# A down-projection by seven products instead of eight

## The chip, the core and the metric

The kernel runs on one core of a Trainium2 chip. The engines are TensorE (PE in the profile), which multiplies matrices, VectorE (DVE) and ScalarE (ACT), which work on elements and read PE's results, GpSimd (POOL), which works on SBUF alone and issues the DMAs that convert types, and SyncE (SP), which issues the others. PE writes into PSUM, eight banks of 512 f32 in each of 128 partitions. The metric is the device time of one execution in microseconds (us); less is better.

## The reference

```
state = gamma * state + k_t v_t^T;  y_t = scale * q_t state        # for each batch (4) and head (8), 768 steps
x  = y as 3072 tokens x 512
xn = x / sqrt(mean(x*x) + 1e-6) * rms_g
out = (silu(xn @ w_gate) * (xn @ w_val)) @ w_out                   # 512 -> 1536 -> 512
```

Inputs and output are f32. A retention layer is followed by a gated feed-forward layer.

## The kernel before

The 768 steps are cut into six chunks `c` of 128 steps; with the four batches `b` a chunk has 512 tokens. Inside a chunk the recurrence becomes a masked product of q and k (operations `A` for the scores, `M0` and `M1` for the mask on DVE, `Y` for the product with v and with the state of the chunks before), and the state is carried from chunk to chunk (`K` the new part on PE, `U` the sum on DVE, `B` a bf16 copy on POOL). `S` and `R` give the norm of each token, `N` scales the rows, and `X` with `XE` or a transposing DMA (`XE` on SP) turns them into `xnT[c]`, with the model dimension on the partitions.

The feed-forward layer then works on 12 blocks `n` of 128 hidden units: `g` and `v` are the gate and value products, four matmuls of 512 tokens for a block (`L549`); `s` is silu on ACT (`L559`); `h` multiplies both on DVE into `hT[c]` (`L567`), 12 blocks x 512 tokens in bf16, of which there are two buffers. The down-projection `d` takes `hT[c]` of one batch (128 tokens) as the stationary operand and a row block of `wo_b` (512 columns) as the moving one, 12 matmuls into one bank (`L574`). `o` copies the bank into SBUF, on DVE or ACT, and `st` stores it (`L587`). For the last batch of the last chunk `e` does the same in three column pieces (`L596`). So the down-projection has 6 x 4 x 12 matmuls of 512 columns, the last 12 of them cut in three.

`H` and `hot` are matmuls of ones, which compute nothing (`L240`, `L234`). `Lq`, `Lk`, `Lv`, `wg`, `wv` and `wo` are loads; `Cq` and `Ck` turn loaded q and k into bf16, `V` does so for v, `D` scales k, `Tq`/`Tk` with `Eq`/`Ek` or `tq`/`tk` transpose.

The order of all this is one string, `ORDER`, written out ahead of the kernel. A word is an operation, its indices, behind `@` its engine (D, A, P, S), and behind `/` its banks: `h.5.0.1.0.4` is chunk 5, block 0 to 1, batches 0 to 4. Each engine takes its instructions in the order of the string, and waits for those of other engines by semaphores, so the string settles what stands behind what in each queue. A bank or a buffer is used again as soon as its last reader is done.

Of the kernel before, what the change touches and what calls it, by code (L numbers as in the profile page):

```python
# [22 lines left out]
N.0.0 M0.0.3 Y.0.1/1 H.1/2 X.0.0/4 J.0.3/7 wv.2.4 S.0.1 XE.0.0@D U.0.0@A R.0.2 R.0.1 Ck.1.1@A N.0.2 B.0.0 H.2/2
Y.0.3/0 g.0.0.2.0.1/2 K.0.2/6 S.0.3 s.0.0.2.0.1 N.0.1 U.0.2@A wg.4.6 X.0.2/4 R.0.3 XE.0.2@D D.0.1@D
v.0.0.2.0.1/3 X.0.1/2 wv.4.6 causal XE.0.1@A Lk.1.2@P v.0.0.2.2.3/4 wg.6.9 Lq.1.2@P wv.6.9 h.0.0.2.0.1
g.0.0.2.2.3/6 D.0.3@D Lq.1.0@P g.0.0.2.1.2/5 g.0.2.3.0.3/3 s.0.0.2.2.3 h.0.0.2.2.3 s.0.0.2.1.2 g.0.3.4.0.3/6
N.0.3 v.0.0.2.1.2/4 D.1.1@D Tq.1.1/5 Lk.1.0@P Tk.1.1/0 X.0.3/7 Eq.1.1@D K.0.1/2 wg.9.12 v.0.3.4.0.3/1 Lv.1.1@P
# [607 lines left out]
```

## Time and profile before

| | |
|---|---|
| three timed runs | 233.72, 233.92, 234.96 us; median 233.92 |
| the profiled execution, first to last instruction (its span) | 233.6 us |
| mean granted PE clock | 0.993 |
| instructions that count as work | PE 1771, DVE 241, ACT 231, POOL 163 |

The profile is one execution; for it there is no time but its span. The busy table gives for each engine the time with an instruction at work, and the slices the same in 40 equal pieces (9 is 90% or more). The chain is followed back from the last instruction, at each step to what released it. In rows of groups, the numbers behind the first bar are the busy time in us and the mean duration in ns, and behind the second the idle time before the group and who ended it. In rows of the timeline and of the chain, the first number is the start and the second the length, in us. A matmul's row in the timeline lasts longer than its share of the stream, since neighbours overlap; the chain counts from end to end.

### The profile page before, as it was taken

To read this page: it belongs to the slowest core of one execution; us is meant where nothing else is said; L and a number is where in the kernel's file an instruction comes from. 1 tells how busy PE (TensorE), PEld (TensorE's weight loads), DVE (VectorE), ACT (ScalarE), POOL (GpSimd) and SP (SyncE) were. 2 spreads that over 40 slices of the span, in tenths; PEclk is the share of its full clock that TensorE was granted. 3 is DMA by queue.
4 is the path that set the end of the run, shared out by engine and by line. 5 is a ranking of instruction groups with operands and counts; after the bars stand their busy time and mean duration, and the time that the engine had idled before them with its cause. 6 is when DMAs were issued, how large, how long until landed. Compare 5 with 4: busy or idle time off the path is not lost.

```text
span 233.6 us, 4637 instructions
## 1 busy us (share of the span) xinstructions
PE 227.6 (97%) x1771; PEld 120.8 (52%) x1771; DVE 130.4 (56%) x241; ACT 96.1 (41%) x231; POOL 89.7 (38%) x163
## 2 busy tenths in 40 slices
PE   8799999999999999999999999999999999999994
PEld 2458855645545655445554444554455444444444
DVE  6479639753662965628975239866367532323320
ACT  7658433514337231464731346553265332232202
POOL 8958998550544555030273741247003100000000
PEclk9979999999999999999999999999999999999999
DMA  7999999999798888999988899968511400020222
GB/s 126 147 180 123 127 179 184 205 145 215 133 206 214 171 194 140 262 218 221 235 173 146 179 221 206 198 149 142 148 61 27 112 0 0 3 90 9 83 89 93
DMA packets 105353, 33.61 MB, mean 144 GB/s; under 512 B 94449, under 2 KB 102385, under 8 KB 105330
## 3 DMA queue, kind: packets, MB, share of 16 engines
q1 hardware_dynamic: 81858, 25.70, 50.2%
q0 software_dynamic: 23472, 7.60, 30.1%
q8 instruction: 14, 0.23, 0.4%
q14 instruction: 9, 0.07, 0.1%
HBM read 28.31 MB, written 6.29 MB: 148 GB/s over the span
## 4 chain that ended last, share of the span: by engine, by line
PE 89%; DMA 4%; POOL 2%; ACT 2%; DVE 1%; issue 0%; SPq 0%; POOLq 0%; DVEq 0%; ACTq 0%
PE v_ps L549 27%; PE g_ps L549 27%; PE o_ps L574 21%; PE a_ps L403 3%; DMA kb<-in_k_dram 3%; PE y_ps L441 2%; PE kv_ps L526 2%; PE y_ps L445 2%; DMA out_dram<-o_sb 1%; PE o_ps L596 1%; PE hot_ps L240 1%; PE t_ps L366 1%; PE t_ps L371 1%; PE xt_ps L495 1%; ACT xsq L455 1%; ACT xsq L458 1%
## 5 line engine op out<-in xcount | busy, mean ns | idle before, releaser
L567 DVE TENSOR_TENSOR hT<-sg,v_ps 128x512 bf16<-128x512 bf16 (+2 forms) x76 | 48.7, 656 | 47.8 <-PE v_ps L549 34.8
L549 PE MATMUL v_ps<-xnT,wv_b 128*128 128x512 bf16 (+2 forms) x344 | 71.2, 345 | 0.1
L559 ACT ACTIVATE sg<-g_ps 128x512 bf16<-128x512 f32 (+2 forms) x76 | 42.1, 575 | 70.6 <-PE g_ps L549 68.1
L549 PE MATMUL g_ps<-xnT,wg_b 128*128 128x512 bf16 (+2 forms) x344 | 70.0, 344 | 0.0
L574 PE MATMUL o_ps<-wo_b,hT 128*128 128x512 bf16 x276 | 63.5, 379 | 0.0
L549 PEld LDWEIGHTS <-wg_b 128*128 128x128 bf16 x344 | 30.4, 98 | 29.3
L549 PEld LDWEIGHTS <-wv_b 128*128 128x128 bf16 x344 | 30.2, 98 | 28.9 <-DVE am L426 0.6
L574 PEld LDWEIGHTS <-hT 128*128 128x128 bf16 x276 | 26.3, 98 | 29.1
L468 POOL TENSOR_SCALAR ms<-ssq 128x1 f32<-128x1 f32 x24 | 4.6, 190 | 59.1 <-ACT xsq L458 58.4
L426 DVE TENSOR_TENSOR am<-a_ps,causal 128x512 bf16<-128x512 f32 x32 | 20.6, 685 | 7.8 <-PE a_ps L403 7.5
L339 POOL TENSOR_TENSOR qb<-qf,ydec 128x512 bf16<-128x512 f32 x13 | 14.0, 1074 | 25.2 <-DMA qf<-in_q_dram 24.9
L146 ACT COPY o_sb<-o_ps 128x512 f32<-128x512 f32 (+1 forms) x16 | 8.8, 552 | 29.7 <-PE o_ps L574 23.1
L458 ACT ACTIVATE xsq<-y_ps 128x512 f32<-128x512 f32 x22 | 13.2, 599 | 18.9 <-PE y_ps L445 13.7
L482 DVE SCALAR_TENSOR_TENSOR xn<-y_ps,rstd,g_bc 128x512 bf16<-128x512 f32 x22 | 16.3, 748 | 4.3 <-POOL rstd L470 3.0
L146 DVE COPY o_sb<-o_ps 128x512 f32<-128x512 f32 (+1 forms) x10 | 6.4, 648 | 18.1 <-PE o_ps L574 12.2
L541 POOL CAST st_b<-st_f 64x256 bf16<-64x256 f32 x40 | 15.9, 398 | 1.3
L470 POOL TENSOR_TENSOR rstd<-ms,mhalf 128x1 f32<-128x1 f32 x24 | 13.3, 552 | 2.0
L534 DVE TENSOR_TENSOR st_f<-st_f,kv_ps 128x512 f32<-128x512 f32 x16 | 10.8, 684 | 5.2 <-PE kv_ps L526 4.6
L356 ACT ACTIVATE vp<-vf,vdec 128x64 bf16<-128x64 f32 x48 | 12.2, 343 | 0.0
L426 DVE TENSOR_TENSOR am<-a_ps,mask 128x512 bf16<-128x512 f32 x16 | 10.4, 686 | 2.5 <-PE a_ps L403 2.3
L240 PE MATMUL hot_ps<-one 128*128 128x512 bf16 x20 | 8.5, 547 | 1.1 <-DVE one L153 1.1
L441 PEld LDWEIGHTS <-am 128*128 128x128 bf16 x176 | 7.8, 99 | 3.1 <-issue 0.3
(99 smaller groups left out, 174.8 us busy)
## 6 DMA issues: line engine op xcount, KB each, us to landing
out_dram<-o_sb SPq DMA_DIRECT2D x23, 256.0 KB, 2.4
kf<-in_k_dram SPq DMA_DIRECT2D x18, 256.0 KB, 3.8
qf<-in_q_dram SPq DMA_DIRECT2D x16, 256.0 KB, 3.9
vf<-in_v_dram SPq DMA_DIRECT2D x16, 256.0 KB, 3.9
wo_b<-in_moe_w_out_dram POOLq DMA_DIRECT2D x3, 512.0 KB, 12.2
qb<-in_q_dram POOLq DMA_DIRECT2D x8, 128.0 KB, 6.6
vp<-in_v_dram POOLq DMA_DIRECT2D x8, 128.0 KB, 6.5
kb<-in_k_dram POOLq DMA_DIRECT2D x6, 128.0 KB, 5.9
```

What stands on the lines that cost most here:

```text
L146: (e.copy if e is ACT else e.tensor_copy)(out, in_)
L339: e.tensor_tensor(out=u["qb"], in0=u["qf"], in1=ydec[:, c, :, None].to_broadcast([128, H, D]), op=ALU.mult)
L426: DVE.tensor_tensor(out=u["am"][:, i], in0=u["a"][i], in1=m, op=ALU.mult)
L441: nc.tensor.matmul(y[:, h, :], u["am"][:, h % 2, h // 2, :], u["vp"][:, h, :], start=h == 0, stop=c == 0 and h == H - 1, skip_group_check= ...
L458: ACT.activation(xsq, flat(u["y"]), AF.Square, accum_out=u["ssq"])
L470: POOL.tensor_tensor(out=u["rstd"], in0=ms, in1=mhalf, op=ALU.pow)
L482: DVE.scalar_tensor_tensor(out=u["xn"], in0=flat(u["y"]), scalar=u["rstd"], in1=g_bc, op0=ALU.mult, op1=ALU.mult)
L541: POOL.tensor_copy(st_b[b][r, :, i * 64:i * 64 + 64], st_f[b][r, :, i * 64:i * 64 + 64])
L549: nc.tensor.matmul(p[:, (n - n0) * m:(n - n0 + 1) * m], W[w][0][:, s, n * 128:(n + 1) * 128], xnT[c][:, s, b0 * C:b1 * C], start=s == 0, s ...
L559: ACT.activation(sg[:, :cols], done["wg", c, n0, b0][:, :cols], AF.Silu)
L567: DVE.tensor_tensor(out=hT[c][:, n0:n1, b0 * C:b1 * C], in0=sg, in1=p, op=ALU.mult)
L574: nc.tensor.matmul(o_ps[c, b], hT[c][:, n, b * C:(b + 1) * C], wo_b[:, n, :], start=n == 0, stop=n == NFF - 1)
```

## The change

For chunks 1 to 5 the down-projection is done by one level of Strassen's method. The left operand, a chunk's 512 tokens x 1536 hidden units, is split in two halves of tokens (batches 0 and 1, `LO`; 2 and 3, `HI`) and two halves of hidden units, and `w_out` in two halves of hidden units and two of columns. The halves of hidden units are interleaved: of each four blocks the first two (`J0`) and the last two (`J1`). Instead of eight products of quarters there are seven; each, for a group of 128 tokens `p` (0 or 1), has six matmuls of 256 columns. They go two to a bank (`ma`, `mb`, `md`) or alone (`m1`; `m6` and `m7` for the very last).

Their left operands are sums of quarters, made for each third `r` of the hidden units: `z1` and `z2` into buffers of their own, `z3` and `z4` in place in `hT`. The right operands `w1`, `w6`, `w7` are made once in buffers, `w3` and `w4` in place in `wo_b`, behind the plain down-projection of chunk 0. The products are put together by `cb` and `c1` (copies out of PSUM), `p1` and `pu` (sum and difference of `ma` with `cb`), `pv` (adds `c1`) and `p2` (adds `md`), and `s1` and `s2` store two halves of 256 columns at a time.

For the room in SBUF, `hT` becomes five buffers of a third of a chunk each; the `w` sums take turns with the masks of chunks 0 and 1 in three buffers (`wide`); `z2` takes turns with `qdec` and `g_row` in four (`mid`), `z1` with `kd`, and the outputs `o1` and `o2` with `o_sb` in five; the squares `xsq` become bf16 with one buffer. The identity is made apart from `pick`. The string `ORDER` is new from end to end: also the loads, the head and the fillers stand in another order. The diff, with the parts of the string that are spoken of below:

```diff
--- before
+++ after
...
-d.5.2.0.12/3 e.5.3.1/0 o.5.1@D st.4.2@S st.5.0@S st.5.1@S e.5.3.2/7 o.5.2@A st.5.2@S o.5.3.2@D st.5.3.2@S
...
+Lk.0.2@S rms.1@S Lq.0.0@P Lq.0.2@P Lq.0.1@P Lk.0.0@P iota Lk.0.1@P ident H.8/0 Ck.0.2@D pick mk1 Lq.0.3@P mk0 vd
+D.0.2@D Tq.0.0/1 Lv.0.2@P Lk.0.3@P G/2 GE@A Lk.1.3@P Tk.0.2/3 Tq.0.2/4 Ek.0.2@D Tk.0.0/5 Lv.0.1@P Tq.0.1/6 Lv.0.3@P
...
+Cq.2.0@P o.0.2@A w7@P w1@P U.1.0@D B.1.0 d.0.1.0.4/7 s.1.10.11.0.4 h.1.8.9.0.4 h.1.1.2.0.3 d.0.0.0.4/3 s.1.2.3.0.3
+A.2.2/1264 M1.2.3 d.0.0.4.8 d.0.1.4.8 tq.2.0 g.1.6.7.0.4/5 M1.2.2 s.1.6.7.0.4 M0.2.3 M0.2.2 d.0.1.8.12 V.2.0@D
+d.0.0.8.12 B.1.1 tk.2.1 Lv.2.1@S A.2.0/4261 o.0.1@D V.2.2@A v.1.2.3.0.3/5 M0.2.1 M1.2.1 B.1.2 M1.2.0 V.2.1@P Lv.2.3@S
+h.1.2.3.0.3 M0.2.0 Y.2.2/7 S.2.2 g.1.3.4.0.3/6 V.2.3@P Y.2.1/1 v.1.6.7.0.4/2 S.2.1 Lk.3.3@S R.2.2 Ck.3.3@P s.1.5.6.0.4
...
+v.1.3.4.0.3/2 h.1.3.4.0.3 z2.1.0@D s.1.9.10.0.4 XE.2.1@S XE.2.3@S Cq.3.3@P Cq.3.2@P v.1.9.10.0.4/6 K.2.3/4 XE.2.0@S
+Lq.4.1@S z1.1.0@D g.1.4.5.0.4/5 K.2.0/2 h.1.9.10.0.4 Lk.3.0@S g.1.7.8.0.4/7 V.3.3@P U.2.3@D Lq.3.1@S v.1.7.8.0.4/6
...
+s.2.9.10.0.4 Lq.4.3@S Lq.4.0@S Cq.4.3@P U.2.0@D v.2.9.10.0.4/7 U.2.2@D z4.1.1@D h.2.9.10.0.4 h.2.7.8.0.4 g.2.6.7.0.4/2
+s.2.6.7.0.4 v.2.5.6.0.4/6 h.2.5.6.0.4 tk.3.3 mb.1.0/3 tq.3.3 Lv.3.1@S mb.1.1/0 tk.3.1 tk.3.0 A.3.2/7426 w3@D cb.1.0@D
+h.2.6.7.0.4 Cq.4.1@D V.3.1@A z4.1.2@D M0.3.3 Lk.4.2@S Lv.3.0@S M1.3.3 B.2.3 Cq.3.1@P B.2.1 B.2.2 g.2.0.1.0.4/3
+g.2.10.11.0.4/5 M0.3.2 M1.3.2 cb.1.1@A s.2.10.11.0.4 g.2.11.12.0.4/0 tq.3.0 v.2.10.11.0.4/2 U.3.3@D g.2.8.9.0.4/6
+tq.3.1 h.2.10.11.0.4 Lq.5.2@S Lk.4.1@S z3.1.1@D z2.2.1@D A.3.0/7541 M1.3.1 B.2.0 s.2.0.1.0.4 V.3.2@A z3.1.0@P
+s.2.8.9.0.4 v.2.8.9.0.4/3 Y.3.2/2 K.3.1/6 Y.3.3/1 M0.3.0 Lq.5.3@S S.3.2 w4@P g.2.2.3.0.4/7 s.2.2.3.0.4 S.3.3 M1.3.0
+M0.3.1 st.0.2@S Ck.4.1@A h.2.8.9.0.4 V.3.0@P Y.3.0/5 Cq.5.2@D K.3.0/4 Ck.5.1@A z1.1.2@D ma.1.0/3 s.2.11.12.0.4 tk.4.0
+Lv.4.3@S tq.4.1 U.3.1@D Y.3.1/7 R.3.2 N.3.2 g.2.1.2.0.4/6 R.3.3 p1.1.0 st.0.1@S pu.1.0 z3.1.2@D ma.1.1/2 v.2.0.1.0.4/0
+S.3.1 Lk.4.3@S st.0.3@S st.0.0@S N.3.3 S.3.0 R.3.0 Ck.4.2@D U.3.0@D v.2.11.12.0.4/3 md.1.0/1 Cq.4.0@D R.3.1 N.3.1
+h.2.11.12.0.4 XE.3.2@S XE.3.3@S N.3.0 pu.1.1 XE.3.1@S md.1.1/4 v.2.3.4.0.4/7 Ck.4.3@P z1.1.1@P m1.1.1/3 p1.1.1
+z3.2.1@P h.2.0.1.0.4 B.3.3 V.4.3@A K.4.3/5 U.4.3@D Lv.4.1@S V.4.1@P XE.3.0@S Lq.4.2@S s.2.1.2.0.4 K.3.2/6
+v.2.2.3.0.4/2 g.2.3.4.0.4/0 s.2.3.4.0.4 h.2.2.3.0.4 U.3.2@D h.2.3.4.0.4 Lv.5.2@S Lv.4.2@S Lk.5.2@S Lq.5.0@S m1.1.0/5
+c1.1.1@D pv.1.1@D Cq.4.2@D c1.1.0@A v.2.1.2.0.4/2 h.2.1.2.0.4 g.3.8.9.0.4/6 s.3.8.9.0.4 p2.1.1 V.4.2@P B.3.1 z4.2.1@D
+g.3.2.3.0.4/0 s1.1.0@S v.3.0.1.0.4/7 Cq.5.3@D v.3.1.2.0.4/3 z2.2.2@D pv.1.0@P z4.2.2@D g.3.1.2.0.4/5 s.3.1.2.0.4
+h.3.1.2.0.4 v.3.8.9.0.4/6 h.3.8.9.0.4 Lv.5.1@S p2.1.0 g.3.0.1.0.4/2 g.3.11.12.0.4/4 K.4.2/5 tk.4.3 s.3.11.12.0.4
...
+h.5.7.8.0.4 z1.5.2@D g.5.4.5.0.4/5 v.5.6.7.0.4/0 z1.4.1@D s.5.6.7.0.4 h.5.6.7.0.4 g.5.5.6.0.4/1 v.5.5.6.0.4/4
+s.5.4.5.0.4 s.5.5.6.0.4 h.5.5.6.0.4 v.5.4.5.0.4/6 h.5.4.5.0.4 z2.5.1@D z3.5.0@D m1.4.1/7 z2.5.2@P z3.5.2@P c1.4.1@A
+z3.5.1@D z4.5.2@D pv.4.1@D p2.4.1 m1.4.0/5 z4.5.1@D c1.4.0@A ma.5.0/0 pv.4.0@D s2.4.1@S s1.4.0@S mb.5.0/1 cb.5.0@A
+p2.4.0 p1.5.0 s1.5.0@S pu.5.0 mb.5.1/4 cb.5.1@A ma.5.1/6 p1.5.1 z1.5.0@P z1.5.1@P m1.5.0/7 s2.4.0@S s1.5.1@S c1.5.0@A
+pu.5.1 pv.5.0@P md.5.0/5 m1.5.1/2 c1.5.1@A p2.5.0 hot.2/1 m6.5.1/3 m7.5.1/4 s2.5.0@S pv.5.1@D p2.5.1.1 s2.5.1.1@S
+p2.5.1.0 H.3/0 hot.3/7 s2.5.1.0@S H.3/6 H.1/1
 """
...
+    def wide(name):
+        return sb.tile([128, 1024], F32, name=name, tag="wide", bufs=3)
+
+    def mid(shape, dtype, name):
+        return sb.tile(shape, dtype, name=name, tag="mid", bufs=MID)
...
-    mask0 = const.tile([128, 2, NHP, C], F32, name="mask0")
-    mask1 = const.tile([128, 2, NHP, C], F32, name="mask1")
-    qdec = const.tile([128, NHP, C], F32, name="qdec")
+    mask0 = wide("mask0").rearrange("p (i hp j) -> p i hp j", i=2, hp=NHP)
+    mask1 = wide("mask1").rearrange("p (i hp j) -> p i hp j", i=2, hp=NHP)
+    qdec = mid([128, NHP, C], F32, "qdec")
...
-    g_row = const.tile([1, DM], F32, name="g_row")
+    g_row = mid([128, DM], F32, "g_row")[0:1]
...
-        xsq = ring([128, DM], F32, "xsq", 2)
+        xsq = ring([128, DM], BF16, "xsq", 1)
...
+    def h_of(c, r):
+        if (c, r) not in hT:
+            hT[c, r] = ring([128, 4, GT], BF16, "hT", HB)
+        return hT[c, r]
...
-    def o(e, bk, c, b, i=None):
-        p = o_ps[(c, b) if i is None else (c, b, i)]
-        if ("o", c, b) not in done:
-            done["o", c, b] = ring([128, DM], F32, "o_sb", 4)
-        copy(e, done["o", c, b] if i is None else done["o", c, b][:, CUT[i]:CUT[i + 1]], p)
-
-    @op
-    def st(e, bk, c, b, i=None):
-        m = slice(0, DM) if i is None else slice(CUT[i], CUT[i + 1])
-        e.dma_start(out=out_v[c, b][:, m], in_=done["o", c, b][:, m])
-
-
-    CUT = (0, 192, 384, 512)
-
-    @op
-    def e(e, bk, c, b, i):
-        p = o_ps[c, b, i] = bank(bk[0], [128, CUT[i + 1] - CUT[i]], F32, "o_ps")
-        for n in range(NFF):
-            nc.tensor.matmul(p, hT[c][:, n, b * C:(b + 1) * C], wo_b[:, n, CUT[i]:CUT[i + 1]],
-                             start=n == 0, stop=n == NFF - 1)
+    def o(e, bk, c, b):
+        done["o", c, b] = ring([128, DM], F32, "o_sb", OB)
+        copy(e, done["o", c, b], o_ps[c, b])
+    @op
+    def st(e, bk, c, b):
+        e.dma_start(out=out_v[c, b], in_=done["o", c, b])
+    wo_q = wo_b.rearrange("p (r j i) m -> p r j i m", j=2, i=2)
+    HM = DM // 2
+    def block(j, m):
+        return wo_q[:, :, j, :, m * HM:(m + 1) * HM]
+    def wsum(i, e, j0, m0, j1, m1, how):
+        if i in (3, 4):
+            x = block(j0, m0)
+        else:
+            x = wide("w%d" % i)[:, :NFF * HM // 4].bitcast(BF16).rearrange("p (r i m) -> p r i m", i=2, m=HM)
+        e.tensor_tensor(out=x, in0=block(j0, m0), in1=block(j1, m1), op=how)
+        done["w", i] = x
+    F["w1"] = lambda e, bk: wsum(1, e, 0, 0, 1, 1, ALU.add)
+    F["w3"] = lambda e, bk: wsum(3, e, 0, 1, 1, 1, ALU.subtract)
+    F["w4"] = lambda e, bk: wsum(4, e, 1, 0, 0, 0, ALU.subtract)
+    F["w6"] = lambda e, bk: wsum(6, e, 0, 0, 0, 1, ALU.add)
+    F["w7"] = lambda e, bk: wsum(7, e, 1, 0, 1, 1, ALU.add)
+    LO, HI = slice(0, GT // 2), slice(GT // 2, GT)
+    J0, J1 = slice(0, 2), slice(2, 4)
+    @op
+    def z1(e, bk, c, r):
+        h = hT[c, r]
+        done["z1", c, r] = sb.tile([128, 2, GT // 2], BF16, name="sA", tag="kd", bufs=4)
+        e.tensor_tensor(out=done["z1", c, r], in0=h[:, J0, LO], in1=h[:, J1, HI], op=ALU.add)
+    @op
+    def z2(e, bk, c, r):
+        h = hT[c, r]
+        done["z2", c, r] = mid([128, 2, GT], BF16, "s2")
+        e.tensor_tensor(out=done["z2", c, r], in0=h[:, J0], in1=h[:, J1], op=ALU.add)
+    @op
+    def z3(e, bk, c, r):
+        h = hT[c, r]
+        e.tensor_tensor(out=h[:, J0, HI], in0=h[:, J0, HI], in1=h[:, J0, LO], op=ALU.subtract)
+    @op
+    def z4(e, bk, c, r):
+        h = hT[c, r]
+        e.tensor_tensor(out=h[:, J1, LO], in0=h[:, J1, LO], in1=h[:, J1, HI], op=ALU.subtract)
+    def left(i, c, p, r, k):
+        h, lo, hi = hT[c, r], slice(p * C, p * C + C), slice(GT // 2 + p * C, GT // 2 + p * C + C)
+        if i == 1:
+            return done["z1", c, r][:, k, lo]
+        if i in (2, 5):
+            return done["z2", c, r][:, k, hi if i == 2 else lo]
+        return h[:, k if i in (3, 6) else 2 + k, hi if i in (4, 6) else lo]
+    def right(i, r, k):
+        if i == 2:
+            return wo_b[:, 4 * r + k, :HM]
+        if i == 5:
+            return wo_b[:, 4 * r + 2 + k, HM:]
+        return done["w", i][:, r, k]
+    def products(name, c, p, bk, which):
+        x = done[name, c, p] = bank(bk[0], [128, len(which), HM], F32, name)
+        for s, i in enumerate(which):
+            for r in range(3):
+                for k in range(2):
+                    nc.tensor.matmul(x[:, s], left(i, c, p, r, k), right(i, r, k),
+                                     start=r == 0 and k == 0, stop=r == 2 and k == 1)
+    F["ma"] = lambda e, bk, c, p: products("ma", c, p, bk, (3, 4))
+    F["mb"] = lambda e, bk, c, p: products("mb", c, p, bk, (5, 2))
+    F["m1"] = lambda e, bk, c, p: products("m1", c, p, bk, (1,))
+    F["md"] = lambda e, bk, c, p: products("md", c, p, bk, (7, 6))
+    F["m7"] = lambda e, bk, c, p: products("m7", c, p, bk, (7,))
+    F["m6"] = lambda e, bk, c, p: products("m6", c, p, bk, (6,))
+    @op
+    def cb(e, bk, c, p):
+        done["cb", c, p] = ring([128, 2, HM], F32, "cb", 2)
+        copy(e, done["cb", c, p], done["mb", c, p])
+    @op
+    def p1(e, bk, c, p):
+        done["o1", c, p] = sb.tile([128, 2, HM], F32, name="o1", tag="o_sb", bufs=OB)
+        DVE.tensor_tensor(out=done["o1", c, p], in0=done["ma", c, p], in1=done["cb", c, p], op=ALU.add)
+    @op
+    def pu(e, bk, c, p):
+        done["o2", c, p] = sb.tile([128, 2, HM], F32, name="o2", tag="o_sb", bufs=OB)
+        DVE.tensor_tensor(out=done["o2", c, p], in0=done["ma", c, p][:, ::-1], in1=done["cb", c, p], op=ALU.subtract)
+    @op
+    def c1(e, bk, c, p):
+        done["c1", c, p] = ring([128, HM], F32, "c1", 1)
+        copy(e, done["c1", c, p], done["m1", c, p][:, 0])
+    @op
+    def pv(e, bk, c, p):
+        o2 = done["o2", c, p]
+        e.tensor_tensor(out=o2, in0=o2, in1=done["c1", c, p][:, None].to_broadcast([128, 2, HM]), op=ALU.add)
+    @op
+    def p2(e, bk, c, p, s=None):
+        o2 = done["o2", c, p]
+        if s is None:
+            DVE.tensor_tensor(out=o2, in0=done["md", c, p], in1=o2, op=ALU.add)
+        else:
+            DVE.tensor_tensor(out=o2[:, s], in0=done[("m7", "m6")[s], c, p][:, 0], in1=o2[:, s], op=ALU.add)
+    def place(c, p, m, s=None):
+        a, b = out_v[c, p][:, m * HM:(m + 1) * HM], out_v[c, p + 2][:, (1 - m) * HM:(2 - m) * HM]
+        if s is not None:
+            return (a, b)[s]
+        return bass.AP(a.tensor, a.offset, (a.ap[0], (b.offset - a.offset, 2), a.ap[-1]))
+    @op
+    def s1(e, bk, c, p):
+        e.dma_start(out=place(c, p, 1), in_=done["o1", c, p])
+    @op
+    def s2(e, bk, c, p, s=None):
+        o2 = done["o2", c, p]
+        e.dma_start(out=place(c, p, 0, s), in_=o2 if s is None else o2[:, s])
```

More of the change, by code (lines that the diff above doesn't have):

```diff
@@ L23 @@
[L23 to L27, printed above, removed]
@@ L563, in h_ @@
         m = (b1 - b0) * C
[L564 to L565 removed]
+        r, i = n0 // 4, n0 % 4
         sg, p = (done[w, c, n0, b0][:, :(n1 - n0) * m].rearrange("p (n t) -> p n t", t=m) for w in ("s", "wv"))
[L567 removed]
+        DVE.tensor_tensor(out=h_of(c, r)[:, i:i + n1 - n0, b0 * C:b1 * C], in0=sg, in1=p, op=ALU.mult)
     @op
```

141 lines of the change are left out of this document (60 added, 81 removed).

## The prediction

> **What bounds the kernel now.** I read the page's busy table and its slices first, then the chain, the waits of the tensor engine (PE), the windows, and last the single rows that price the edits.
>
> ```profile
> PE 227.6 (97%) x1771; PEld 120.8 (52%) x1771; DVE 130.4 (56%) x241; ACT 96.1 (41%) x231; POOL 89.7 (38%) x163
> PE   8799999999999999999999999999999999999994
> PEclk9979999999999999999999999999999999999999
> PE 89%; DMA 4%; POOL 2%; ACT 2%; DVE 1%; issue 0%; SPq 0%; POOLq 0%; DVEq 0%; ACTq 0%
> PE t_ps L366 <- DMA kb<-in_k_dram: 1.4, 2, 1.0
> PE hot_ps L240 <- DVE one L153: 1.1, 1, 1.1
> 100.00:120.00 20.00, 20.00 (x158) 10.60 (x157) 14.44 (x23) 12.05 (x34) 5.93 (x13) 1.00 1.01 226
> 140.00:160.00 20.00, 19.88 (x192) 10.76 (x186) 16.15 (x28) 11.38 (x37) 7.26 (x16) 1.00 0.89 178
> 200.00:220.00 20.00, 20.00 (x94) 9.11 (x93) 7.21 (x11) 5.85 (x10) 0.00 (x0) 1.00 0.11 40
> ```
>
> PE is busy 97% at a full granted clock except in the third slice; it is 89% of the chain; and its two waits, 2.5 us, both lie at the very start. The last three rows (columns: window, length, then PE, weight loads, DVE, ACT, POOL) say that even where VectorE (DVE) is busy 16.15 of 20 us, PE loses only 0.12 us. So time is PE work, and a busy DVE is not yet a bound. A change is worth the PE work that it removes, less what it makes PE wait for.
>
> **The price of PE work.**
>
> ```profile
> 20.43 0.45 PE v_ps L549 x8
> 61.12 0.65 PE v_ps L549 x4
> 91.14 2.59 PE o_ps L574 x12
> 220.04 7.77 PE o_ps L574 x36
> 227.81 2.66 PE o_ps L596 x36
> ```
>
> In the chain, eight matmuls of 128 columns take 0.45 us (0.056 each), four of 384 take 0.65 (0.1625), twelve of 512 take 2.59 (0.216), each with a weight load of its own. That is a straight line, 0.0533 us for each 128 columns, so 256 columns, which the trace does not have, come to 0.109. The weight load is not a floor: it is there at 0.056 too. Removed: 276 matmuls at 0.216 and the 36 of the last row, 59.6 + 2.66 = 62.2. Added: 48 whole ones for chunk 0 (10.4) and, for five chunks, 2 token groups x 7 products x 6 matmuls = 420 at 0.109 (45.8), 56.2 in all. **Saved: 6.0 us**, all on the path if PE keeps busy. All other PE work has the same counts in both orders.
>
> **Fillers and head.**
>
> ```profile
> L240 PE MATMUL hot_ps<-one 128*128 128x512 bf16 x20 | 8.5, 547 | 1.1 <-DVE one L153 1.1
> 11.10 0.66 PE a_ps L403 x16
> ```
>
> The 20 wide fillers are all in the head now; the new order puts 13 there and 7 behind the last product, where they run beside the last store. The first attention scores now start at 11.10. POOL, which issues the loads, no longer makes the identity and the row mask before its first load; but the first matmuls after the fillers wait for loads all the same, and behind the first scores the head runs through the same S, R, N, X steps. I take -0.5 us; bounds -2 (seven fillers at 0.216 and some waiting) and +2 (a cold clock, or weights that come later behind the early load of k of chunk 1).
>
> **What is added on the other engines.**
>
> ```profile
> L567 DVE TENSOR_TENSOR hT<-sg,v_ps 128x512 bf16<-128x512 bf16 x64 | 42.8, 685 | 44.6 <-PE v_ps L549 31.6 <-ACT sg L559 12.6
> L482 DVE SCALAR_TENSOR_TENSOR xn<-y_ps,rstd,g_bc 128x512 bf16<-128x512 f32 x22 | 16.3, 748 | 4.3 <-POOL rstd L470 3.0 <-ACT sg L559 1.2
> L146 DVE COPY o_sb<-o_ps 128x512 f32<-128x512 f32 x9 | 6.1, 687 | 14.6 <-PE o_ps L574 12.2 <-DMA out_dram<-o_sb 2.4
> L567 DVE TENSOR_TENSOR hT<-sg,v_ps 128x256 bf16<-128x256 bf16 x4 | 1.7, 417 | 1.8 <-PE v_ps L549 1.7
> L146 DVE COPY xnT<-xt_ps 128x512 bf16<-128x512 bf16 x5 | 2.1, 422 | 2.1 <-PE xt_ps L495 2.1
> L517 DVE TENSOR_TENSOR kd<-kb,vdec 128x512 bf16<-128x512 bf16 x3 | 2.1, 686 | 0.3 <-ACT vdec L259 0.3
> L517 POOL TENSOR_TENSOR kd<-kb,vdec 128x512 bf16<-128x512 bf16 x2 | 2.1, 1035 | 0.1
> 113.36 0.69 DVE L426 TENSOR_TENSOR am<-a_ps,causal 128x512 bf16<-128x512 f32 x1
> 113.97 0.68 DVE L358 TENSOR_TENSOR vp<-vf,vdec 128x512 bf16<-128x512 f32 x1
> ```
>
> From 113.36 to 113.97 is 0.61: in a row, a DVE operation of 0.685 costs 0.61 (0.07 overlaps). p1, pu, pv and p2 work on 512 floats: 0.61 on DVE, pv 1.04 on POOL. The four sums z1, z3, z4 (512) and z2 (1024) have no row: both inputs and the output are bf16 in SBUF. The far ends are kd, 686 ns (0.61), whose second input vdec is f32, and the all-bf16 copy, 422 ns (0.35). Every 685 row has an f32 operand; the sums have none, so I take 0.35 and, for z2, 0.62; slow ends 0.61 and 1.15. The Trainium skill (VectorE: DVE Perf Modes, The perf-mode tier table) gives bf16 tensor_tensor in SBUF two elements a cycle; by it the sum is the one with the fast end, and no row of this trace shows it.
>
> What does it load? In the new order the densest stretch runs from `g.2.6.7` to `p2.1.0`, the products of chunk 1. PE work there, counted: 22 wide gate and value groups of four matmuls at 0.216 (19.0), 84 product matmuls at 0.109 (9.2), and attention (3.8): 32.0 us. DVE: 11 h, 8 mask products, 5 state sums, 5 qb, 2 p1, 2 pu, 2 p2, 1 pv, 1 cb (37 at 0.61 = 22.6), 4 xn (2.7), 6 small sums (2.1), 2 z2 (1.2), w3 (0.9), kb and c1 (0.35 each, as the 422 and 417 rows: 0.7) are 30.2, with 0.8 for starts after a wait **31 of 32 us**. With slow sums it is 6 x 0.26 + 2 x 0.53 + 0.8 more, 34.4. DVE hid everything at 16.15 of 20; at 31 of 32 it cannot, for it also waits in here for PE (`h.2.0.1` reuses the buffer of chunk 1's first rows and so comes behind `md.1.1`) and for DMA: `pu.1.0`, `pu.1.1` and `p1.1.1` take buffers of chunk 0's outputs and wait until these are stored. Behind them on DVE are the h of chunk 2, which free PE's banks, and the stores lie on SP behind loads and transposes. How full it can be here no row shows, only that 81% costs nothing; I estimate 91 to 94%, which makes 33 to 34 us: **+2.0 us**, bounds 0 and 6.2 (34.4 at 90%). From there on DVE has 24 of 32 us in the next products, and nothing is added.
>
> ```profile
> 125.31 0.68 DVE L358 TENSOR_TENSOR vp<-vf,vdec 128x512 bf16<-128x512 f32 x1
> 125.52 1.37 POOL L339 TENSOR_TENSOR qb<-qf,ydec 128x512 bf16<-128x512 f32 x1 [2.22 <-DMA qf<-in_q_dram]
> 129.75 1.04 POOL L339 TENSOR_TENSOR qb<-qf,ydec 128x512 bf16<-128x512 f32 x1 [2.85 <-DMA qf<-in_q_dram]
> 80.41 1.04 POOL L358 TENSOR_TENSOR vp<-vf,vdec 128x512 bf16<-128x512 f32 x1
> 81.40 0.85 POOL L541 CAST st_b<-st_f 64x256 bf16<-64x256 f32 x2
> ```
>
> POOL gets w7 and w1, 1536 elements each, three times a kd: 3.1 each. They stand between `Cq.2.0` and `B.1.0`; behind them wait three B (0.8 each, last row) and `V.2.1`, which `Y.2.1` needs: 1.04 + 6.2 + 2.4 + 1.04 = 10.7 us of POOL, for 8.9 us of PE work up to there. POOL is late by 1.8 if it is on time before: **+0.8 us**, half of it, since it may start early; bounds 0 and 2.5. ACT gives 15 of 16 o and takes 6 cb and 6 c1: no change. A POOL operation also grows: under a DVE operation with two SBUF inputs (overlap 0.47 us) qb took 1.37 for 1.04, 0.7 us for each us of overlap. The Trainium skill (GPSIMD Engine Reference, Specifications) says that POOL's SBUF interfaces are shared with VectorE and contended by DVE instructions with two SBUF inputs; the trace agrees, 1.37 against 1.04.
>
> **The tail.**
>
> ```profile
> 230.50 0.32 ACT L146 COPY o_sb<-o_ps 128x192 f32<-128x192 f32 x1 [1.29 <-PE o_ps L596]
> out_dram<-o_sb SPq DMA_DIRECT2D x23, 256.0 KB, 2.4
> out_dram<-o_sb SPq DMA_DIRECT2D x2, 96.0 KB, 1.7
> ```
>
> Behind the last value matmul stand 10.4 us of PE now (7.77 + 2.66) and 10.5 then (96 at 0.109). DVE has in that time one h, z2, two z3, two z4, 3 pv, 2 p1, 2 pu, 3 whole p2 and a half one, about 9.1 us (10.6 slow) before the last half p2: just in time. The end is then 0.42 for a half p2 (the 256-column row) instead of 0.32, and a store of 128 KB, between 1.7 and 2.4: **+0.25 us** (0.2 to 1.5). The stores carry as many bytes as before, most in rows of half the length; with a DMA share of 0.11 of one (window from 200) that costs nothing late.
>
> **Sum.** The profiled execution has a span of 233.6; the median of the three timed runs is 233.92, 0.3 above it. 233.6 - 6.0 - 0.5 + 2.0 + 0.8 + 0.25 = 230.15, and with 0.3 about **230.4 us**.
>
> **Rivals.** (1) *All of the gain arrives*: DVE stays within its lead and POOL starts early, so both waits are 0 and the head gives up to 2: 233.6 - 6.0 - 2 + 0.2 + 0.3 = 226.1 to 228. For it: PE lost nothing at 16.15 of 20. Against: 31 of 32.
>
> (2) *DVE becomes the bound, slower than before.* If the bf16 sums run at kd's 0.61, the stretch needs 34.4 / 0.9 = 38.2 us for 32 of PE work (+6.2), the 10 us of PE work before `g.1.4.5`, counted in the same way, have 9.9 of DVE, some 1 more, and the tail 1.5: 233.6 - 6.0 - 0.5 + 6.2 + 1 + 0.8 + 1.5 + 0.3 = 236.9. It decides as soon as the waits together pass 6.2 us. For it: the kd row; against: the 422 of all-bf16 rows.
>
> (3) *POOL is late* by the sharing of the port. The two-input SBUF operations of DVE fill some 9 of the 32 us (8 z, 5 qb, w3, pv), which lengthens POOL's 20 us there by 20 x 9/32 x 0.7 = 3.9; with 2.0 for w7 and w1: 233.6 - 6.0 - 0.5 + 2.0 + 3.9 + 2.0 + 0.25 + 0.3 = 235.6 if each is waited for, about 233 if half is. Against: POOL has room, 20 of 32.
>
> (4) *The products do not halve*: if 256 columns cost 0.120 or more, 420 x 0.011 = 4.6 of the 6.0 are lost: 235.0. Against: the straight line.
>
> **How the numbers follow.** Forecast 0.52, (1) 0.20, (2) 0.13, (3) 0.10, (4) 0.05. Half a per cent, about what a measurement here can tell from none, is 1.2 us: 232.75 to 235.1. Forecast and (1) are faster (the forecast's own range 228 to 232.5), and some of (3): 0.74. Same: most of (3) and (4), 0.11. Slower: (2) and the rest, 0.15. The range from 226.3 to 236 leaves out the upper half of (2) and the lowest edge of (1).
>
> **What would show it.** Right: z rows of 128x512 on DVE at about 0.42 us and z2 at 0.7; six products in 0.65 us in the chain; PE idle 2 to 3 us in all behind DVE and POOL, around chunk 1's products and `Y.2.1`. Wrong: z at 0.69 and DVE in the chain for over 5%; POOL rows of 1.3 us and more, with PE behind them; a head that is over 2 us longer; product matmuls of 0.12 us and more.

## The result, and the profile after

The changed kernel takes 241.68 us (median of 4 runs, 240.54 to 243.80), the kernel before 233.84 beside it: 1.033 times as long (95% interval 1.027 to 1.039). The forecast was 230.4, with 236.0 as the upper end. Of the runs further down, one execution of `nov` (246.3), one of `sums_dve` (253.1) and two of `old34` (246.6, 247.3) were slow ones, at a lower granted clock and over 1.5% above the fastest of their kernel, and the medians leave them out. The page of the changed kernel, whose profiled execution took 241.23 us:

```profile
PE 223.5 (93%) x1927; PEld 137.5 (57%) x1927; DVE 178.3 (75%) x312; ACT 95.6 (40%) x233; POOL 143.2 (60%) x194
PE   6989999999499999986999989999999999999895
PEclk9999999999999999999999999999999999999999
PE 45%; DVE 6%; DMA 5%; issue 3%; POOL 3%; SPq 3%; ACT 0%; DVEq 0%; ACTq 0%
```

PE does less work at a full clock, but it now has holes in the slices 11, 18 and 19, and is 45% of the chain instead of 89%. DVE has 48 us more than before, POOL 54. The waits of PE (us in total, times, longest), the five longest:

```profile
PE g_ps L562 <- DVE st_f L547: 3.6, 1, 3.6
PE y_ps L454 <- DVE am L439: 2.3, 2, 1.8
PE t_ps L379 <- DMA qb<-in_q_dram: 1.2, 1, 1.2
PE hot_ps L250 <- DVE one L163: 1.1, 1, 1.1
PE g_ps L562 <- ACT cb L150: 1.0, 1, 1.0
```

The two longest are new, and both end on DVE. The timeline shows what stood in front, first around 61, then around 106 us (rows of PE, DVE and POOL):

```profile
60.45 7.03 POOL L616 TENSOR_TENSOR w<-wo_b 128x1536 bf16<-128x1536 bf16 x2
61.23 3.30 DVE L150 CAST kb<-kf 128x512 bf16<-128x512 f32 x1
64.45 0.68 DVE L547 TENSOR_TENSOR st_f<-st_f,kv_ps 128x512 f32<-128x512 f32 x1
65.18 1.02 PE L562 MATMUL g_ps<-xnT,wg_b 128*128 128x512 bf16 x4 [3.56 <-DVE st_f L547]
...
104.27 3.09 POOL L616 TENSOR_TENSOR wo_b<-wo_b 128x1536 bf16<-128x1536 bf16 x1
105.59 2.05 DVE L643 TENSOR_TENSOR hT<-hT 128x512 bf16<-128x512 bf16 x1
107.32 1.23 POOL L371 TENSOR_TENSOR vp<-vf,vdec 128x512 bf16<-128x512 f32 x1
107.57 1.53 DVE L638 TENSOR_TENSOR s<-hT 128x1024 bf16<-128x1024 bf16 x1
...
109.75 0.39 PE L454 MATMUL y_ps<-vp,am 128*128 128x64 bf16 x8 [1.80 <-DVE am L439]
```

A cast of 0.42 us took 3.30, a sum of 0.42 took 2.05, one of 0.69 took 1.53; each lies beside an operation of POOL and ends 0.3 to 0.6 us behind the end of one (104.27 + 3.09 = 107.36 and 105.59 + 2.05 = 107.64). Behind them in DVE's queue stood the state sum and the masks that PE waited for.

For the balance I take a profile of the kernel before whose time is known (233.24 us, span 231.4, a later run). Counting the matmuls that had started by a given time, each at its price from the prediction (0.03 for 64 columns), by their weight loads where a matmul's own row is missing, and without fillers, PE had done, in us of work:

| by | 20 | 60 | 70 | 100 | 115 | 150 | 220 | last product ends | span |
|---|---|---|---|---|---|---|---|---|---|
| before, again | 11.3 | 51.1 | 61.4 | 91.9 | 107.0 | 142.6 | 212.8 | 227.9 | 231.4 |
| after | 9.0 | 49.1 | 55.4 | 85.5 | 97.3 | 131.5 | 201.4 | 234.5 | 239.3 |

So 2.0 us are lost by 60, 4.0 between 60 and 70, 3.3 between 100 and 115, 1.4 more by 150, little behind that but some 1.2 at the very end, and 1.3 between the last product and the end. That is 12.6 + 1.3 of loss against 6.0 of saved work: 7.9 us of span.

### The profile page after: what moved, and what is told of

The parts are those of the page before. It is cut to its first block, busy times and chain, and to the rows that moved or that the text cites. A ratio compares the mean times of both kernels' runs of the same rounds, so it can differ in the third digit from the quotient of the medians.

```text
span 239.3 us, 5041 instructions
## 1 busy us (share of the span) xinstructions
PE 223.5 (93%) x1927; PEld 137.5 (57%) x1927; DVE 178.3 (75%) x312; ACT 95.6 (40%) x233; POOL 143.2 (60%) x194
## 4 chain that ended last, share of the span: by engine, by line
PE 45%; DVE 6%; DMA 5%; issue 3%; POOL 3%; SPq 3%; ACT 0%; DVEq 0%; ACTq 0%
PE g_ps L562 14%; PE v_ps L562 13%; PE mb L671 5%; PE md L671 4%; PE ma L671 4%; PE m L671 2%; DVE hT L584 2%; DMA qT<-qb 2%; SPq L400 1%; DMA qf<-in_q_dram 1%; DVE xn L495 1%; PE a_ps L416 1%; DMA xnT<-xn 1%; DVE am L439 1%; SPq L514 1%
## 5 line engine op out<-in xcount | busy, mean ns | idle before, releaser
L671 PEld LDWEIGHTS <-hT 128*128 128x128 bf16 x240 | 23.1, 98 | 5.9 <-POOL hT L648 0.8
L638 POOL TENSOR_TENSOR s<-hT 128x1024 bf16<-128x1024 bf16 x6 | 13.2, 2200 | 18.8 <-DVE hT L584 18.8
L471 ACT ACTIVATE xsq<-y_ps 128x512 bf16<-128x512 f32 x22 | 13.1, 597 | 18.6 <-PE y_ps L458 17.2
L352 POOL TENSOR_TENSOR qb<-qf,ydec 128x512 bf16<-128x512 f32 x10 | 10.3, 1042 | 14.7 <-DMA qf<-in_q_dram 14.6
L648 POOL TENSOR_TENSOR hT<-hT 128x512 bf16<-128x512 bf16 x7 | 8.1, 1170 | 15.7 <-DVE s L638 15.5
L671 PE MATMUL ma<-wo_b,hT 128*128 128x256 bf16 x120 | 14.9, 273 | 0.4 <-DVE hT L584 0.3
L671 PE MATMUL mb<-wo_b,s 128*128 128x256 bf16 x120 | 14.4, 272 | 0.0
L671 PE MATMUL md<-w,hT 128*128 128x256 bf16 x108 | 13.1, 273 | 0.5 <-POOL hT L648 0.5
L371 POOL TENSOR_TENSOR vp<-vf,vdec 128x512 bf16<-128x512 f32 x8 | 8.5, 1066 | 8.1 <-DMA vf<-in_v_dram 8.1
L671 PEld LDWEIGHTS <-s 128*128 128x128 bf16 x120 | 11.7, 98 | 2.4
```

The source lines that it names most:

```text
L352: e.tensor_tensor(out=u["qb"], in0=u["qf"], in1=ydec[:, c, :, None].to_broadcast([128, H, D]), op=ALU.mult)
L471: ACT.activation(xsq, flat(u["y"]), AF.Square, accum_out=u["ssq"])
L638: e.tensor_tensor(out=done["z2", c, r], in0=h[:, J0], in1=h[:, J1], op=ALU.add)
L671: nc.tensor.matmul(x[:, s], left(i, c, p, r, k), right(i, r, k), start=r == 0 and k == 0, stop=r == 2 and k == 1)
```

## The experiments

Theory A: DVE's operations that work in SBUF stand still while POOL works, and PE waits behind them. Rivals: B, DVE is full by its own work; C, POOL is late; D, the matmuls behind the last product delay the end. A fifth, F, came up on the way. All times below are medians; the kernel before took 233.7 to 234.2 beside them.

**probe.** Behind the last store of the changed kernel:

```
+for pool in ("add", "cast"):                  # POOL: 1536 elements, two inputs, or one
+    for f in kinds:                           # DVE: two of a kind
+        DVE.tensor_copy(va, ps); POOL's operation on va; DVE add that reads ps
+        f(); f()
```

> The changed kernel with a measuring block behind its last store, which lengthens the span by some 40 us and computes nothing that is used. In the block POOL runs one operation of 1536 elements (an add of two bf16 inputs, then a cast with one input), VectorE (DVE) first an operation that reads PSUM, 0.68 us, and then twice one kind: nothing, bf16 add, f32 add, bf16 + f32 add, cast f32 to bf16, scalar_tensor_tensor in bf16, and an add that reads PSUM, all 512 wide and in SBUF but the last. Theory A (a DVE operation that needs the port shared with POOL stands still until POOL's operation is done): beside POOL's add, which took 3.1 to 3.8 us, the first of the two takes 2 to 3 us instead of 0.42 or 0.68, the second its own time; the one that reads PSUM stays at 0.68. Open within A: whether only the 0.42 kinds (bf16 add, cast) stand still, or every kind with two SBUF inputs; and whether POOL's cast, with one input, does the same. Rival (DVE was only overloaded, the long rows come from elsewhere): all kinds keep 0.42 or 0.68 and POOL's operation grows instead.

The timeline of the block, DVE behind POOL's add and behind its cast (each x2 row is two of a kind, the x3 row holds the PSUM add ahead too):

```profile
245.59 3.08 POOL L740 TENSOR_TENSOR wv_b<-wv_b 128x1536 bf16<-128x1536 bf16 x1 [0.80 <-DVE wv_b L753]
246.02 3.39 DVE L740 TENSOR_TENSOR wg_b<-wg_b 128x512 bf16<-128x512 bf16 x2
250.53 3.92 DVE L740 TENSOR_TENSOR wg_b<-wg_b 128x512 f32<-128x512 f32 x2
260.60 3.39 DVE L746 CAST wg_b<-wg_b 128x512 bf16<-128x512 f32 x2
265.10 3.92 DVE L747 SCALAR_TENSOR_TENSOR wg_b<-wg_b 128x512 bf16<-128x512 bf16 x2
269.54 2.00 DVE L740 TENSOR_TENSOR wg_b<-wg_b,probe_ps 128x512 bf16<-128x512 bf16 x3
...
275.83 1.47 POOL L757 CAST wv_b<-wv_b 128x1536 bf16<-128x1536 f32 x1 [0.79 <-DVE wv_b L753]
276.28 1.75 DVE L740 TENSOR_TENSOR wg_b<-wg_b 128x512 bf16<-128x512 bf16 x2
```

Every kind that takes two inputs from SBUF, or casts within SBUF, stood still until POOL was done: two bf16 sums took 3.39 us (0.42 + 0.35 = 0.77 alone), with their end 0.74 us behind POOL's, two f32 sums 3.92, of which 1.27 lie behind POOL's end. The three that read PSUM took 2.00, 0.67 each, so nothing was added. POOL's add kept its 3.08. So DVE does stand still as theory A has it, and it matters neither whether DVE works in bf16 or f32 nor how many inputs POOL has. The Trainium skill (SBUF — State Buffer, Who interferes with whom) says just this: such a DVE instruction and POOL take the shared pair of ports for a whole instruction, and whoever comes second stands still; the trace agrees for DVE as the second, 3.39 against 0.77. The block has no case of POOL as the second.

**w_dve** (`w7@P w1@P` at 60 us taken out; `w7@D` ahead of the masks of chunk 2, `w1@D` behind `z4.1.1@D`), **sums_dve** (`z1..z4@P`, `w4@P` -> `@D`, all in place) and **no_fill** (`- H.3/0 hot.3/7 ... H.3/6 H.1/1`, behind the last product):

> w7 and w1 on DVE, in places where DVE was idle (ahead of the masks of chunk 2, and behind z4.1.1), 0.9 us each there, instead of 7.0 us on POOL; nothing else is changed. Theory A (DVE's SBUF operations stand still behind a POOL operation in progress, and PE behind DVE): the cast of k that took 3.30 us takes 0.4, PE's gap of 3.56 us at 65 is gone, and B and V on POOL come 7 us earlier: 241.7 - 3 to - 4 = 238. Rival B (DVE is simply full): 2 us more on DVE bring nothing or cost up to 2 us: 241 to 244. Rival C (POOL late by w7 and w1 was the matter): also some 238, but with the cast still long.

> All 25 sums of hidden units that POOL had (19 of 512, 6 of 1024) and w4 on DVE, each at its place in the order; w7 and w1 stay on POOL. This takes 39 us from POOL and gives DVE 19 x 0.35 + 6 x 0.62 + 0.9 = 11.3 us more. Theory A: the sums that took 0.8 to 2 us beside POOL's sums take 0.42 and 0.69, about 8 of the 13 us of DVE's lengthening go, and the gaps at 103 and 110 shrink: 237 to 240. Rival B (DVE is full as it is): PE waits for DVE by a good part of the 11.3 us, in the stretch of chunk 1's products above all: 244 to 250.

> Without the 7 wide matmuls of ones and the 7 small ones behind the last product. Theory D (they delay the end of the program, beside the last store): the time from the last product to the end falls, and the 1.9 us between span and timed run fall to the 0.2 of the kernel before: 240. Rival: nothing is changed, 241.7, the 1.9 us have another cause; if they keep PE's clock up for nothing behind them, also 241.7.

Measured: 243.96, 246.25 and 242.43. D is out: 242.4 against 241.7. w_dve and sums_dve lie where rival B put them, and not where A did. Of w_dve the waits of PE show the first gap small, and others in its place:

```profile
PE y_ps L454 <- DVE am L439: 2.5, 2, 1.9
...
PE v_ps L562 <- DVE hT L584: 1.9, 3, 1.5
...
PE g_ps L562 <- DVE st_f L547: 0.7, 1, 0.7
```

It was not the move of w7 and w1 that did this. no_fill is the changed kernel up to its last product, with w7 and w1 on POOL, and its first gap is 0.7 too (its waits for `am`, `hT` and `st_f` are 2.6, 1.8 and 0.7). There the cast of k was ahead of w7 on the shared ports:

```profile
60.91 1.27 DVE L150 CAST kb<-kf 128x512 bf16<-128x512 f32 x1
61.86 6.33 POOL L616 TENSOR_TENSOR w<-wo_b 128x1536 bf16<-128x1536 bf16 x2
```

Who comes first differs between executions of the same order: the gap is 3.6 in the changed kernel and 3.1 in probe, 0.7 in no_fill and nov, and the cast takes 1.27 in w_dve as in no_fill. Nor is the gap worth its length. Counted as in the table above, no_fill had done 58.0 us of work by 70, 2.6 more than the changed kernel, but 94.8 by 115, 2.6 less; w_dve is within 0.5 of no_fill throughout. So what w7 and w1 on POOL cost is not shown by w_dve.

With sums moved to DVE the time grows by four tenths of the work moved (4.6 us for 11.3). A alone does not fit, and neither does C: a wait that is taken away comes back elsewhere. So something else was close behind. I took the change apart.

**plain_order, no_pool_sums, no_sums, skip1.**

```
plain_order:   ma.c.p -> d.c.p.0.12, md.c.p -> d.c.(p+2).0.12, p1 -> o@D, p2 -> o@A; no z, w, mb, m1
no_pool_sums:  z, w on POOL: return, the products read wv_b or block(j0, m0) in their place
no_sums:       the same for all z and w
skip1:         chunk 1 as in plain_order; h.0.5.6.0.3 w6@D w7@D w1@D; w3, w4 @D behind the h of chunk 3
```

> The changed kernel in its new order and with its new buffers, but with the plain down-projection in all chunks: where ma stood the 12 matmuls of batch p, where md stood those of batch p + 2, their copies on DVE and ACT, no sums and no other products. If the sums and products are what costs (theory of a full DVE): as the kernel before, 233 to 234.5. Rival (the order, its head or the five thirds of hT cost time by themselves): 236 and more.

> Leaves out the sums that POOL makes (25 of hidden units, and w7, w1, w4); the products read weights or unsummed blocks in their place, and all else is as in the changed kernel. DVE makes the same sums as before. If DVE's wait for POOL's operations is what costs (about 10 of the 13 us by which DVE's operations are lengthened stand behind POOL's sums): 235 to 237. If DVE is full by its own work alone, and POOL's sums only run beside it: 240 to 242.

> Leaves out all sums, on DVE too (60 of hidden units, the five w); products, assembly and stores are as in the changed kernel. If the sums with what they make wait are the whole loss: 233.9 - 6.0 and a little at the tail, 228 to 229.5. If the assembly (p1, pu, pv, p2, cb, c1: 30 us on DVE and POOL for 13 us of copies before) or the order is a part of it: 231 to 235.

> The plain down-projection in chunk 1 too, products in chunks 2 to 5; w6, w7, w1 on DVE in a gap of 5.9 us that DVE has behind the h of chunk 0 at 52 us, w3 and w4 on DVE behind the h of chunk 3; the sums of chunks 2 to 5 stay where they are. PE saves 4 x 1.2 = 4.8 us instead of 6.0. If a full DVE around the products of chunk 1 costs the 6 to 7 us that PE loses between 60 and 116: 229.5 to 232.5, faster than the kernel before. If the loss only moves to the next chunk: 236 to 239.

Measured: 247.99, 236.79, 239.07, 243.04. no_pool_sums came out as expected of the wait for POOL; no_sums and skip1 lie above all that I had expected, and plain_order by its rival, and by far. The new order costs 14 us with the plain down-projection, and without any sum the kernel still takes 239. Why without DVE's sums it took rather longer than without POOL's (239.1, 236.8) I can't say; the runs overlap (237.0 to 240.1, 236.4 to 238.0). What PE waits for in plain_order:

```profile
PE a_ps L407 <- DMA qT<-qb: 3.9, 2, 2.2
PE v_ps L553 <- DMA xnT<-xn: 1.9, 1, 1.9
PE y_ps L445 <- POOL vp L362: 1.3, 1, 1.3
```

And in no_sums, the timeline of SP, POOL and PE around the first such wait:

```profile
67.21 1.22 SPq L400 DMA_TRANSPOSE kT<-kb  x1
68.53 1.21 SPq L400 DMA_TRANSPOSE qT<-qb  x1
69.83 1.22 SPq L400 DMA_TRANSPOSE kT<-kb  x1
71.09 1.20 SPq L327 DMA_DIRECT2D vf<-in_v_dram  x2
...
74.63 1.04 POOL L371 TENSOR_TENSOR vp<-vf,vdec 128x512 bf16<-128x512 f32 x1 [7.47 <-DMA vf<-in_v_dram]
...
75.73 0.39 PE L454 MATMUL y_ps<-vp,am 128*128 128x64 bf16 x8 [1.27 <-POOL vp L371]
```

SP issues one DMA behind the other without a pause, and v comes last: PE is ready for `Y.2.1` at 74.5 and waits for it. Here is theory F: the new order starts the attention of chunk 2 at 66 us here (70 in the changed kernel) where the kernel before starts it at 75 (`A.2.0`) and 81 (`A.2.2`), and its loads don't come that much earlier. v of batch 1 is issued at 71.1 here and at 70.9 in the kernel before, but `Y.2.1`, which reads it, stands there at 81.6. In the kernel before PE waits for no load behind the head (its two waits are in the prediction, both at the start), so there the loads of v had nothing to give. The next runs cross both causes.

**nov, no_sums_nov, v_act** (nov: `load` of v for chunks 2 to 5 -> `t[c, b]["vf"] = g_bc`; v_act: `Lv.2 .. Lv.5 @S -> @A`, `Lv.2.1`, `Lv.2.3` behind `Lv.2.0`), and later **nov_no_pool** (nov and no_pool_sums together):

> The changed kernel without the 16 loads of v of chunks 2 to 5 (the scaling of v reads a constant tile in their place), which takes some 10 us of issue from SP and 4 of 33 MB from the DMA engines; sums and products stay. Theory F (the new order asks for the loads and transposes of chunks 2 and 3 some 10 us earlier than the kernel before, while SP issues without a pause, 9.2 to 9.6 us of every 10 from 50 to 110, as without the sums too): the waits for the scaled v at 75 and for transposed q at 98 to 145 go; DVE's waits stay: 236 to 239. Rival (DVE and its waits for POOL alone): 241 to 242, as DVE does the same.

> Leaves out all sums and the 16 loads of v of chunks 2 to 5. Theory F: with neither DVE nor the loads behind, PE loses little after 20 us, 239.1 - 7 = 230 to 233. Rival (the rest of the loss is of the assembly on DVE and ACT, or of the order in banks): 236 to 239.

> The 16 loads of v of chunks 2 to 5 issued by ACT instead of SP, those of chunk 2 together, the result as before. If SP's issuing is the pace of theory F: 237 to 240. If it is the DMA engines (their share of busy time is 0.7 to 1.0 there), nothing is won: 241 to 243; if ACT stands still behind a full buffer, slower.

> Without the 16 loads of v of chunks 2 to 5 and without the sums that POOL makes (25 of hidden units, w7, w1, w4); DVE makes its own 35 sums, w6 and w3. With the loads out of the way, 238.0 with all sums and 230.4 with none are the ends. If DVE's standing still behind POOL's sums (and their being late) makes the 7.6 us: 231 to 233. If DVE's own sums and assembly fill it: 236 to 238.

| | all sums | without POOL's | without any |
|---|---|---|---|
| all loads | 241.7 | 236.8 | 239.1 |
| without the loads of v | 237.9 | 232.1 | 230.4 |

Taking away the loads alone gives 3.8 us, all sums alone 2.6, both 11.3. Each hides the other: whichever is left makes PE late in the same stretch. From 70 to 150 us PE did 76 us of work in the changed kernel, 75 in nov and 72 in no_sums, but 81 in no_sums_nov, as many as in the kernel before. No single removal could have shown that. That no_sums_nov comes to the forecast's 230.4 is chance: it has nothing of the 2.8 us that the forecast gave to waits for DVE and POOL, and a longer head. With the loads away, POOL's sums are worth 5.8 of the 7.5 us and DVE's own 35 sums 1.8 (1.2 by the ratios to the kernel before that ran beside each). The pages of nov and nov_no_pool show how:

```profile
PE 223.5 (95%) x1927; PEld 137.9 (58%) x1927; DVE 177.6 (75%) x312; ACT 95.9 (41%) x233; POOL 142.3 (60%) x194
PE 221.3 (96%) x1900; PEld 138.1 (60%) x1927; DVE 168.0 (73%) x312; ACT 95.7 (42%) x233; POOL 98.8 (43%) x166
```

The same 312 DVE operations take 9.6 us less (a sum that is left out also can't make a product wait for it). In nov PE waits 3.0 us once for the masks behind the sums; in nov_no_pool its longest such wait is 0.5:

```profile
PE y_ps L457 <- DVE am L442: 3.5, 2, 3.0
...
PE y_ps L457 <- DVE am L442: 0.5, 1, 0.5
```

PE's clock has a part in this. A row of windows gives the stretch, its length, PE's busy time, and third from its end the granted clock, first for nov, then for nov_no_pool:

```profile
105.00:110.00 5.00, 3.35 (x34) 2.49 (x34) 5.00 (x9) 1.38 (x4) 1.63 (x4) 0.78 0.91 212
...
105.00:110.00 5.00, 4.86 (x59) 3.58 (x57) 5.00 (x10) 3.84 (x11) 1.70 (x4) 1.00 0.80 191
```

In the next 5 us nov has 0.88. By an estimate from these windows that is up to 1.1 + 0.6 = 1.7 us of PE work lost in and behind the wait. w_dve and no_fill have 0.66 from 110 to 115, plain_order 0.71 from 105 to 110, v_act 0.50 from 70 to 75, each in or just behind a window in which PE stood still for 1 us or more; the changed kernel kept 1.00 through its gaps of 3.6 and 1.8. So a wait can cost more than its length, and need not. The table doesn't hang on it: the execution of nov with a mean clock of 0.999 took 237.06, those of nov_no_pool at 1.000 took 231.2 to 232.4.

v_act took 246.71, though SP had room (it issued nothing from 77.2 to 86.3): ACT sat idle 6.8 us around the issues of chunk 2, and silu came late (PE waited 3.0 us once for it). Whether SP's queue or the DMA engines set the pace is not settled by it.

**old4, old34, old4b, old45.** If both causes lie in what stands beside the products, these must pay where no loads, no attention and no POOL work are left: in the order of the kernel before, from 185 us on. All sums on DVE, six thirds of `hT`, buffers of their own for all w.

```
old4:   d.4.0 -> mb.4.0 cb, d.4.1 -> ma.4.0 p1 pu, d.4.1.10 -> mb.4.1 cb, d.4.0.10 -> ma.4.1 p1 pu,
        d.4.3 -> m1.4.0 c1 md.4.0 pv, d.4.2 -> m1.4.1 c1 md.4.1 pv; z2 behind the last h of each third
old34:  the same in chunk 3; md.3.0, md.3.1 behind g.4.11, g.4.0
old4b:  - ma.4.1/6 p1.4.1 pu.4.1 ... h.5.2.3 h.5.4.5    + ma.4.1/6 ... h.5.2.3 h.5.4.5 p1.4.1 pu.4.1
old45:  d.5.0, d.5.2 -> z of 128 + 128 tokens, mb.5.0 ma.5.0 m1.5.0 md.5.0 behind d.5.1; e.5.3 last
```

> The order of the kernel before, with products in chunk 4 alone: its sums and w on DVE, where DVE had 1 to 3 of 5 us, POOL almost nothing and SP no loads left; the last chunk stays plain, with the old end. PE saves 1.2 us. Theory F + A (products pay where neither the loads nor DVE's waits behind POOL are near PE): 232.4 to 233.2. Rival (the sums and assembly cost PE as much anywhere, or the new buffers do): 233.8 to 235.

> The same with products in chunks 3 and 4; all sums on DVE, md of chunk 3 behind the first products of chunk 4's hidden units. PE saves 2.4 us. Theory: 231.4 to 232.6, if DVE, 4.7 of 5 us busy around 150, keeps ahead; rival: the waits for DVE there (POOL works there too) take it back, 233 to 235.5.

> As old4, but p1 and pu of the second token group of chunk 4 behind the h of block 4 of chunk 5 on DVE, since in old4 PE waited 1.1 us for the h that stood behind them (its bank). That wait gone: 234.5 - 1.1 = 233.4, 0.3% under the kernel before. If the wait only moves: 234.5.

> As old4b, and in chunk 5 the batches 0 and 2 by products too (sums of 128 + 128 tokens alone), behind the plain batch 1; batch 3 stays last and in three pieces, so that the end is the old one. PE saves another 0.6 us: 232.4 to 233.2. If the sums of the last third come late behind the last h: 234 and more.

Measured: 234.49, 244.00, 233.15, 232.62. old4 gave back what it saved; its waits named one new one, which old4b took away:

```profile
PE g_ps L556 <- DVE hT L578: 1.1, 1, 1.1
```

old34 missed by 11 us, and its rival's range by 8. It puts the sums among the masks and norms of the next chunk's attention, where the plain down-projection had been work for PE on rows of `hT` that were long made; its single causes I have not taken apart. old45 leaves nothing out and beats both kernels, by little: 0.994 of the time before (0.991 to 0.997). Its page:

```profile
PE 223.3 (97%) x1801; PEld 125.5 (54%) x1825; DVE 147.7 (64%) x278; ACT 97.6 (42%) x235; POOL 89.4 (39%) x163
PE 81%; DMA 7%; POOL 6%; DVE 2%; issue 2%; ACT 1%; POOLq 0%; DVEq 0%; ACTq 0%
```

**before_again**, the kernel before unchanged:

> The kernel before, for a profile whose own time is known: 1.9 to 2.0 us above its span, as in all runs whose span is known, that is a span of 231.5 to 232.6 for 233.5 to 234.6, not 233.6.

233.24 us with a span of 231.4: 1.9 us lie around the span, not 0.3 (1.7 to 2.2 in the timed executions of all runs). By that the profile that the prediction used was of an execution of some 235.5 us, 1.6 above the median, with its lost time at the start: PE had done 8.6 us of work by 20 in it, 11.3 in this one.

## Why the prediction was wrong, step by step

- **PE work: right.** In the chain 24 product matmuls take 2.62 us and six 0.66, 0.109 each; the 6.0 us are there (62.28 less 56.15 is 6.1), as no_sums_nov shows, where almost nothing is lost between 20 us and the last product (230.4).

```profile
96.97 2.62 PE mb L671 x24
121.45 0.66 PE m L671 x6
```

- **"All other PE work has the same counts in both orders": the step that failed first.** The count is right, but moved work needs its data at its new time. The prediction costed no load and no transpose of the moved attention, and had no term for SP outside the head and three buffers. With the sums left out, the loads of v alone are worth 8.7 us (239.1 against 230.4), where PE in the kernel before waited for none of them.
- **The dense stretch, +2.0: mis-sized, and for another reason.** From `g.2.6.7` to the gate product of chunk 3's block 0, which stands behind `p2.1.0`, PE had 32.0 us of work; 33 to 34 us, as the prediction estimated, would be 1 to 2 more, of which it took the upper end. The stretch took 35.7; 37.1 in nov, but 32.6 in nov_no_pool and 32.2 in no_sums_nov. So DVE, busy for 30.5 of the 32.6 us in nov_no_pool, cost 0.4 us with its own sums, less than forecast, and POOL's sums 4.5 more, of which up to 1.7 are the clock's, by the estimate above.
- **The price of contention was put on the wrong engine.** The prediction had seen qb on POOL grow from 1.04 to 1.37 under a DVE operation and charged POOL, 0.7 us for each us of overlap. That is the case in which DVE came first. With POOL first, DVE waits for the rest of an operation of up to 3 us, and DVE was the fuller queue. Rival (3) had the mechanism's half; its time, 235.6, fell short.
- **The sums alone: right.** z1, z3, z4 take 0.41 at least and z2 0.68, as forecast, and yet their mean is longer (columns: busy us, mean ns):

```profile
L638 DVE TENSOR_TENSOR s<-hT 128x1024 bf16<-128x1024 bf16 x9 | 8.0, 888 | 0.1
L632 DVE TENSOR_TENSOR sA<-hT 128x512 bf16<-128x512 bf16 x10 | 6.9, 702 | 0.0
L643 DVE TENSOR_TENSOR hT<-hT 128x512 bf16<-128x512 bf16 x8 | 5.9, 750 | 0.0
L150 DVE CAST kb<-kf 128x512 bf16<-128x512 f32 x5 | 5.0, 1009 | 0.6 <-DMA kf<-in_k_dram 0.6
```

- **POOL late by w7 and w1, +0.8: the place was right, the victim wrong.** They took 7.03 us; what stood still was DVE's cast, and PE lost 3.56 in this execution, 0.72 in those of no_fill and nov, where the cast came first.
- **Head, -0.5: +2.0**, the upper bound: by 60 us PE has done 49.1 instead of 51.1. That is against the execution of 233.24 us, which is nearer to the median; in the longer one that the prediction read it was 49.1 too.
- **Tail, +0.25: +1.3.** c1 has one buffer, so the last c1 waited for pv on POOL (2.14 us idle), and the last pv and p2 for both:

```profile
232.76 1.27 POOL L704 TENSOR_TENSOR o<-o,c 128x512 f32<-128x512 f32 x1 [5.27 <-ACT c L150]
234.07 0.37 ACT L150 COPY c<-m 128x256 f32<-128x256 f32 x1 [2.14 <-POOL o L704]
235.46 0.76 DVE L712 TENSOR_TENSOR o<-m,o 128x256 f32<-128x256 f32 x2
```

- **Around the span, 0.3: 1.9.** It all but cancels, since the profile before was 1.6 us above the median.
- **Rivals.** (2) named a side that came true, slower behind DVE, by a cause that did not: kd's 0.61 for each sum. (4) is out by the 0.109.
